# A limit on the weight bytes under way in a recurrent attention chain

## The chip, the cores and the metric

The kernel runs on one core of one Trainium2 chip. The metric is the device time of one execution in microseconds (us). The core has a matrix engine (TensorE, "PE" in the profile, its weight loads "PEld"), three engines for other arithmetic (VectorE "DVE", ScalarE "ACT", GpSimd "POOL"), and SyncE ("SP"), which here does nothing but issue transfers between the chip's memory (HBM) and the on-chip memory. SP issues the large transfers and POOL the small ones; all of them are carried by the same 16 DMA engines. A transfer that has ended raises a semaphore, and instructions wait on semaphores.

## The reference, cut to what matters

Four layers are applied in turn, A, B, A, B, each to the layer-normed rows and added to them:

```python
for s in range(n_seg):                        # layer A: 64 segments of 32 tokens
    h = concatenate([mem, x[32*s:32*s+32]])   # 8 memory rows + 32 tokens, 640 wide
    q, k, v = h @ Wq, h @ Wk, h @ Wv          # 32 heads of 192: 6144 columns each
    p = softmax(mask(q @ k.T * scale))
    o = (p @ v) @ Wo                          # back to 640 columns
    mem = o[:8]                               # the memory of the next segment
    outs.append(o[8:])
```

The eight memory rows make layer A a chain: a segment's projections can't start before the segment before it has gone through `Wo`. Layer B is a linear attention over all 2048 rows and isn't touched here. All weights are bf16; `Wq`, `Wk`, `Wv` and `Wo` together have 31.5 MB, more than the on-chip memory holds.

## The kernel before

Each A layer has two parts. `A_pre` computes the queries, keys and values of the last eight tokens of every segment ahead of time and stores them in HBM (`kqb_d`, `vb_d`). `A_chain` then runs the 64 segments one after another, in an order of instructions written out by hand on every engine.

**Rounds.** The 32 heads are taken in four rounds of eight heads, in the order 0, 1, 2, 3 in even segments and 3, 2, 1, 0 in odd ones. A round projects Q, K and V (`project`, L988; the input rows are stationary and the weights stream through), forms scores (`scores`, L1025 and L1030), weighs them (L1085, L1099, L1104 to L1106), multiplies with the values (`attend`, L1038) and goes through its quarter of `Wo` (`wo_round`, L1067: 12 steps of four matmuls, in the order of the columns of the weight tile). The sum over the four rounds is turned (L1220) and copied into the next segment's input `hT` (L1221, two copies). In what follows a segment begins at the end of the second copy.

**Streamed weights.** Most of the weights stay on chip. What doesn't fit is shared by the first and the last round of a segment: three of the five 128-row blocks of each of Q, K and V have one slot, and the tile `wo_end` holds a quarter of `Wo` for round 0 or round 3. When the first round has used a slot, SP issues the transfer that fills it for the last round. Per segment SP issues 18 transfers, always in this order, which is also the order of the names used below:

| name | tile and line of the issue | KB each |
|---|---|---|
| Q1 to Q3 | `slot["Q"]`, L681 | 384 |
| K1 to K6 (halves) | `slot["K"]`, L681 | 192 |
| V1 to V3 | `slot["V"]`, L681 | 384 |
| w1 to w6 | `wo_end` from `wo_rows`, L698 | 320 |

The transfer of a slot waits for the matmuls that read the slot before. There are also eight completion semaphores, used in turn, so a transfer waits for the one issued eight places earlier. SP takes its instructions in order. Q1 is issued 0.09 us after a segment begins, V3 at 6.8 us and w6 at 11.7 us (medians of the trace). The last round of `Wo` reads w1 to w6 in order; its matmuls 41 to 48 read w6.

**Small transfers.** POOL issues, in each segment, four loads of the precomputed values (`extra_v`, L971, `Vp<-vb`, 28 KB), four of the precomputed keys and queries (`load_kqb`, L959, 48 KB), four stores of tails (`store_tail`, L1058, 24 KB), one load of rows (L939) and one store (L955). Two tiles `Vp` are used in turn, so the load for round n + 2 is issued when `attend` of round n is done. The load for the last round, the second of the segment and called Vp1 below, is issued 12.1 us into the segment, and `attend` of the last round waits for it.

PE also fetches its own instructions by transfers of 16 KB on a queue of its own ("q8 instruction" in the page).

Of the kernel before, what the change touches and what calls it, by code (L numbers as in the profile page):

```python
# [8 lines left out]
P = 128  # L9
# [10 lines left out]

FILL = {0: 86, 2: 79}
SEG_FILL = 2

LATE = 64512
ARENA = 202752
# [90 lines left out]
class Kernel:  # L116
# [526 lines left out]
    def layer_A(self, xn_dram, at_dram, li, x_raw=None):  # L643
        nc, tc = self.nc, self.tc
        KC, NSEG = self.KC, self.NSEG
        dram = self.dram
        NR = 4
        PW = 1536
        self.kqb_d = dram.tile([NR, P, NSEG, 192], BF16, name=f"kqb{li}")
        self.vb_d = dram.tile([NSEG, NR, 2, 8, 896], BF16, name=f"vb{li}")  # L650
        self.otb_d = dram.tile([P, NSEG, 384], BF16, name=f"otb{li}")
        wview = self.wview
        wov = self.A_Wo.rearrange("h d m -> (h d) m").rearrange("(c p) m -> p c m", p=P)
        low = self.view(0, LATE)
        at = LATE
        res, slot = {}, {}
        for r in (3, 2):
            for m in "KQV":
                for b in range(KC - (SLOTS[m] if r == 3 else 0)):
                    res[m, r, b] = low[:, len(res) * PW:len(res) * PW + PW]  # L660
        assert len(res) * PW * 2 == LATE
        for m, r, b in [(m, 0, b) for m in "KQV" for b in range(KC - SLOTS[m])] + \
                [(m, None, b) for m in "KQV" for b in range(KC - SLOTS[m], KC)] + [(m, 1, b) for m in "KQV" for b in range(KC)]:
            v = self.view(at, 2 * PW)
            at += 2 * PW
            if r is None:
                slot[m, b] = v
            else:
                res[m, r, b] = v
        holds = {}  # L670
        wo_mid = self.view(at, 24 * 1280)
        wo_end = self.view(at + 24 * 1280, 12 * 1280)
        assert at + 36 * 1280 == ARENA
        unread = set(res)

        def load_slot(m, r, b, whole=False):
            if holds.get((m, b)) != r:
                holds[m, b] = r
                w = PW if whole or m in "QV" else PW // 2
                for h in range(0, PW, w):  # L680
                    nc.sync.dma_start(out=slot[m, b][:, h:h + w], in_=wview[m][:, b, PW * r + h:PW * r + h + w])  # L681

        def load_matrix(m, r):
            for b in range(KC):
                if (m, r, b) in unread:
                    unread.remove((m, r, b))
                    nc.sync.dma_start(out=res[m, r, b], in_=wview[m][:, b, PW * r:PW * r + PW])
                elif (m, r, b) not in res:
                    load_slot(m, r, b, True)

        early = {(0, 4), (0, 5), (2, 4), (2, 5), (1, 0), (1, 1), (1, 2), (1, 3)}

        def load_wo(r, into=None, part=range(6)):
            t = into if into is not None else wo_end[:, :] if r in (0, 3) else wo_mid[:, 7680 * (r - 1):7680 * r]
            for k in part:
                tk = t[:, 1280 * k:1280 * k + 1280]
                if r in (0, 3):
                    self.last_load = nc.sync.dma_start(out=tk, in_=self.wo_rows[r // 3, :, 1280 * k:1280 * k + 1280])  # L698
                else:
                    nc.sync.dma_start(out=tk.rearrange("p (c m) -> p c m", m=640),  # L700
                                      in_=wov[:, 12 * r + 2 * k:12 * r + 2 * k + 2, :])

        def piece(m, r, b):
            assert (m, r, b) in res or holds[m, b] == r
            return res[m, r, b] if (m, r, b) in res else slot[m, b]

        if li == 0:
            self.wo_rows = dram.tile([2, P, 7680], BF16, name="wo_rows")

        def lay_out_wo(i):  # L710
            nc.sync.dma_start(out=self.wo_rows[i].rearrange("p (c m) -> p c m", m=640), in_=wov[:, 36 * i:36 * i + 12, :])

        def early_wo():
            for r in (2, 0, 1):
                load_wo(r, part=[k for k in range(6) if (r, k) in early])

        def late_wo(r, part=range(6)):
            load_wo(r, part=[k for k in part if (r, k) not in early])

        self.A_pre(xn_dram, li, load_matrix, piece, wo_mid, wo_end, lay_out_wo, early_wo, x_raw)  # L720
        self.A_chain(xn_dram, at_dram, li, load_slot, piece, load_wo, late_wo, wo_mid, wo_end, low)
        self.post_args = at_dram, wo_mid, wo_end, low

# [192 lines left out]
    def A_chain(self, xn_dram, at_dram, li, load_slot, piece, load_wo, late_wo, wo_mid, wo_end, low):  # L916
# [3 lines left out]
        with tc.tile_pool(name=f"A{li}_ch", reuse_waits="tile", bufs=1) as sp, \  # L920
# [150 lines left out]
            def keep_busy(ps, n, w=384):  # L1071

                for _ in range(n):
                    nc.tensor.matmul(ps[:, 0:w], lhsT=self.ident[:, :], rhs=wo_mid[:, 0:w], start=True, stop=True,  # L1074
                                     skip_group_check=True)

            def fill(n):

                for _ in range(n):
                    nc.tensor.ldweights(self.ident[:, 0:1])  # L1080
# [40 lines left out]
            for s in range(NSEG):  # L1121
# [93 lines left out]
                keep_busy(idle, 5, 230)  # L1215
                fill(SEG_FILL)
                if s + 1 < NSEG:
# [87 lines left out]
```

## Time and profile before

| | us |
|---|---|
| median of three runs (3610.51 to 3611.67) | 3610.64 |
| span of the profiled execution, first to last instruction | 3590.5 |
| what lies around the span (no time of its own is listed for the profiled execution, so this is against the median) | 20.1 |
| 62 segment periods of the first A layer and 62 of the second, in sum | 2621.6 |
| mean, median and fastest twentieth of a segment period | 21.14, 21.01, 20.71 |

The two chains take 73% of the span. PE is marked busy for 97% of the span, but that share says little: matmuls are pipelined and a dependent step shows as a gap of tenths of a microsecond. What matters is which event ends last before each step of a segment, so the chain of work that ended last, the waits and the landing times of transfers are read segment by segment.

### The profile page before, as it was taken

The numbers are of one execution on the slowest core, as the hardware profiler recorded it, in microseconds if no ns is written. First come the engines' busy times: TensorE is split into PE (matmuls) and PEld (weight loads), VectorE is DVE, ScalarE is ACT, GpSimd is POOL, SyncE is SP. The second block draws the span as 40 slices with busy tenths as digits, with TensorE's granted clock in tenths as the row PEclk, the third lists the DMA queues.
The fourth block names the chain that finished last, engine by engine and source line by source line (L and its number), as shares of the span: only waits on it lengthen the run. The fifth ranks groups of instructions, "written<-read, shape, count | busy, mean of one in ns | idle before, by whom it ended". The sixth has DMA issues, their size and how long they took to land.

```text
span 3590.5 us, 168460 instructions
## 1 busy us (share of the span) xinstructions
PE 3465.5 (97%) x70978; PEld 2268.6 (63%) x71399; DVE 2327.0 (65%) x6320; ACT 2032.0 (57%) x5233; POOL 1589.1 (44%) x4173
## 2 busy tenths in 40 slices
PE   9989999999999999999999899999999999999999
PEld 7756666666666666655377566666666666666553
DVE  5466666667666666746633566666666666676465
ACT  3356666666566656646432556666666666666463
POOL 3445555555555555530123455555545555555400
PEclk9999999999999999999999999999999999999999
DMA  8988888888788878860476878887888888888600
GB/s 311 334 290 288 281 295 282 278 292 299 278 284 295 289 277 278 295 224 3 146 272 217 290 275 287 290 291 278 285 294 279 290 282 292 292 281 287 222 1 30
DMA packets 452689, 929.38 MB, mean 259 GB/s; under 512 B 75338, under 2 KB 218330, under 8 KB 448858
## 3 DMA queue, kind: packets, MB, share of 16 engines
q1 hardware_dynamic: 382266, 817.56, 64.0%
q0 software_dynamic: 67744, 87.80, 7.9%
q8 instruction: 557, 9.13, 1.0%
q10 hardware_dynamic: 1920, 13.24, 0.9%
q14 instruction: 202, 1.65, 0.1%
HBM read 848.50 MB, written 73.73 MB: 257 GB/s over the span
## 4 chain that ended last, share of the span: by engine, by line
PE 55%; DMA 20%; issue 9%; DVE 7%; POOL 5%; ACT 4%; SPq 1%; PEld 0%; POOLq 0%; ACTq 0%; DVEq 0%
PE ps_qk L988 17%; DMA arena<-wo_rows 7%; DMA Vp<-vb 6%; PE ps_v L988 6%; PE ps_w L1067 6%; PE ps_pre L878 3%; PE ps_o L1038 3%; PE ps_s L1030 3%; DVE hT L943 2%; PE ps_s L1099 2%; DMA arena<-in_A_Wv_dram 2%; PE ps_s L1025 2%; PE ps_pre L902 2%; PE ps_idle L1074 2%; PE kv L1260 1%
## 5 line engine op out<-in xcount | busy, mean ns | idle before, releaser
L988 PEld LDWEIGHTS <-hT 128*32 128x32 bf16 x30720 | 746.5, 96 | 431.9 <-DVE hT L1221 27.2
L988 PE MATMUL ps_qk<-arena,hT 128*32 128x384 bf16 x20480 | 998.8, 328 | 14.6 <-DMA arena<-in_A_Wq_dram 4.2
L998 ACT ACTIVATE raw<-ps_qk 128x384 bf16<-128x384 f32 x1024 | 502.0, 490 | 383.7 <-PE ps_s L1099 250.9
L988 PE MATMUL ps_v<-arena,hT 128*32 128x384 bf16 x10240 | 534.6, 328 | 8.7 <-DMA arena<-in_A_Wv_dram 8.4
L971 POOL DMA_DIRECT2D Vp<-vb x512 | 258.4, 505 | 611.4 <-PE ps_o L1038 465.6
L1067 PE MATMUL ps_w<-arena,OT 128*32 128x160 bf16 x18432 | 446.1, 234 | 11.4 <-DMA arena<-wo_rows 10.4
L1003 DVE STREAM_TRANSPOSE KT<-raw 128x384 bf16<-128x384 bf16 x512 | 296.0, 578 | 194.5 <-ACT raw L998 190.5
L1067 PEld LDWEIGHTS <-OT 128*32 128x32 bf16 x18432 | 322.7, 96 | 103.8 <-ACT OT L1044 22.3
L1006 DVE STREAM_TRANSPOSE QT<-raw 128x256 bf16<-128x256 bf16 x512 | 227.9, 445 | 237.5 <-ACT raw L998 195.5
L959 POOL DMA_DIRECT2D kqb<-kqb x512 | 290.9, 568 | 168.9 <-POOL KT L967 147.3
L1019 DVE CAST Vp<-ps_v 64x384 bf16<-64x384 f32 x512 | 286.2, 559 | 113.6 <-ACT Vp L1017 90.0
L1106 DVE TENSOR_TENSOR E<-E,ps_s 80x320 bf16<-80x320 bf16 x512 | 247.4, 483 | 142.7 <-ACT ps_s L1105 142.3
L1058 POOL DMA_DIRECT2D otb<-otb x512 | 282.7, 552 | 128.1 <-DVE otb L1054 100.0
L1017 ACT ACTIVATE Vp<-ps_v 64x384 bf16<-64x384 f32 x512 | 246.1, 481 | 138.4 <-PE ps_v L988 122.9
L1038 PEld LDWEIGHTS <-Vp 80*128 80x128 bf16 x4096 | 189.9, 99 | 123.1 <-issue 80.5
L1038 PE MATMUL ps_o<-E,Vp 80*128 80x80 bf16 x4096 | 233.0, 201 | 31.8 <-DMA Vp<-vb 15.0
L1085 ACT ACTIVATE E<-ps_s 80x320 bf16<-80x320 f32 x512 | 221.4, 432 | 68.0 <-PE ps_s L1030 33.6
L951 ACT ACTIVATE Vp<-ps_w 32x160 bf16<-32x160 f32 x512 | 150.3, 294 | 155.1 <-DVE wt L1220 138.4
L964 POOL COPY QT<-kqb 128x64 bf16<-128x64 bf16 x512 | 124.5, 243 | 254.8 <-PE ps_s L1030 248.5
L1030 PE MATMUL ps_s<-QT,KT 128*80 128x80 bf16 (+1 forms) x3072 | 233.2, 213 | 1.6 <-POOL KT L967 1.5
L1104 ACT ACTIVATE ps_s<-ps_s 80x320 f32<-80x320 f32 x512 | 214.7, 419 | 31.2 <-PE ps_s L1099 31.2
L1030 PEld LDWEIGHTS <-KT 128*80 128x80 bf16 x3072 | 205.4, 119 | 28.7 <-issue 18.3
(156 smaller groups left out, 5446.4 us busy)
## 6 DMA issues: line engine op xcount, KB each, us to landing
arena<-wo_rows SPq DMA_DIRECT2D x780, 320.0 KB, 6.8
arena<-in_A_Wq_dram SPq DMA_DIRECT2D x427, 384.0 KB, 4.4
arena<-in_A_Wv_dram SPq DMA_DIRECT2D x427, 384.0 KB, 6.6
arena<-in_A_Wk_dram SPq DMA_DIRECT2D x768, 192.0 KB, 4.6
kqb<-kqb POOLq DMA_DIRECT2D x512, 48.0 KB, 5.1
arena<-in_A_Wk_dram SPq DMA_DIRECT2D x43, 384.0 KB, 7.8
vb<-arena POOLq DMA_DIRECT2D x128, 112.0 KB, 6.3
Vp<-vb POOLq DMA_DIRECT2D x512, 28.0 KB, 4.8
```

The lines of the kernel that those rows point to most:

```text
L959: nc.gpsimd.dma_start(out=kqb[:], in_=self.kqb_d[r, :, s, :])
L971: nc.gpsimd.dma_start(out=Vs[n % 2][64:80, :], in_=self.vb_d[s, r].rearrange("g t f -> (g t) f"))
L988: nc.tensor.matmul(o[32 * g:32 * g + 32, 0:384], lhsT=hT[:, b, :], rhs=rhs, start=(i == 0), stop=(i == KC - 1), tile_position=(0, 32 * g), ...
L998: nc.scalar.activation(out=raw[:], in_=ps[:, 0:384], func=ACT.Copy)
L1003: nc.vector.transpose(out=KT[:, :, 0:64], in_=raw[:, :].rearrange("p (c j) -> p c j", j=64))
L1017: nc.scalar.activation(out=o, in_=i, func=ACT.Copy)
L1019: nc.vector.tensor_copy(out=o, in_=i)
L1030: nc.tensor.matmul(S[0:80, c0:c0 + 80 * (q1 - q0)], lhsT=KT[:, 3 * x + i, :], rhs=QT[:, x, q0:q1, :], start=False, stop=(x == 1 and i == 2 ...
L1038: nc.tensor.matmul(O[x][:, 80 * i:80 * i + 80], lhsT=Vs[n % 2][0:80, 448 * x + k:448 * x + k + 128], rhs=E[0:80, 160 * x + 80 * e:160 * x ...
L1058: nc.gpsimd.dma_start(out=self.otb_d[:, s, 96 * r:96 * r + 96], in_=otb[:, :, :].rearrange("p c t -> p (c t)"))
L1067: nc.tensor.matmul(W[32 * g:32 * g + 32, 0:160], lhsT=OT[:, c, q:q + 32], rhs=w[:, 640 * i + 160 * g:640 * i + 160 * g + 160], start=(firs ...
L1106: nc.vector.tensor_tensor(out=E[0:80, 0:320], in0=E[0:80, 0:320], in1=rc, op=ALU.mult)
```

## The change

Inside `A_chain`, each transfer of a streamed weight is entered in a list with its bytes. Going back from the newest one, the bytes are added up, its own included; the first transfer with which the sum passes 1,310,720 bytes (1.25 MB) must have completed before the new one is issued. The wait stands on SP, ahead of the issue. Transfers of `A_pre`, of resident weights and of layer B aren't entered, nor are POOL's. The order of instructions is the same on every engine.

```diff
+FLIGHT = 1310720
...
         holds = {}
+        under_way = []
+        self.pacing = False
+
+        def stream(out, in_, nbytes):
+
+            load = nc.sync.dma_start(out=out, in_=in_)
+            if self.pacing:
+                under_way.append((load.ins, nbytes))
+                total = 0
+                for ins, n in reversed(under_way):
+                    total += n
+                    if total > FLIGHT:
+                        tc.add_manual_dep(load.ins, ins.name,
+                                          mybir.DependencyInfo(mybir.DependencyClass.Sync, mybir.DependencyReason.DATA),
+                                          reason="few streamed weights under way")
+                        break
+            return load
+
...
                 for h in range(0, PW, w):
-                    nc.sync.dma_start(out=slot[m, b][:, h:h + w], in_=wview[m][:, b, PW * r + h:PW * r + h + w])
+                    stream(slot[m, b][:, h:h + w], wview[m][:, b, PW * r + h:PW * r + h + w], 2 * P * w)
...
                 if r in (0, 3):
-                    self.last_load = nc.sync.dma_start(out=tk, in_=self.wo_rows[r // 3, :, 1280 * k:1280 * k + 1280])
+                    self.last_load = stream(tk, self.wo_rows[r // 3, :, 1280 * k:1280 * k + 1280], 2560 * P)
...
         self.A_pre(xn_dram, li, load_matrix, piece, wo_mid, wo_end, lay_out_wo, early_wo, x_raw)
+        under_way.clear()
+        self.pacing = True
         self.A_chain(xn_dram, at_dram, li, load_slot, piece, load_wo, late_wo, wo_mid, wo_end, low)
```

With the sizes of the table the rule gives these pairs, a transfer and the one that it waits for: K1 and K2 for Q1, K3 and K4 for Q2, K5 and K6 for Q3, V1 for K2, V2 for K4, V3 for K6, w1 for V1, w2 for V2, w3 and w4 for V3, w5 for w1, w6 for w2. Q1 to Q3 wait for w4 to w6 of the segment before.

## The prediction

> **What bounds the kernel now.** I read the chain that ended last first: it tells which events a segment waits for. From the page:
>
> ```profile
> span 3590.5 us, 168460 instructions
> PE 55%; DMA 20%; issue 9%; DVE 7%; POOL 5%; ACT 4%; SPq 1%; PEld 0%; POOLq 0%; ACTq 0%; DVEq 0%
> PE ps_qk L988 17%; DMA arena<-wo_rows 7%; DMA Vp<-vb 6%; PE ps_v L988 6%; PE ps_w L1067 6%; PE ps_pre L878 3%; PE ps_o L1038 3%; PE ps_s L1030 3%; DVE hT L943 2%; PE ps_s L1099 2%; DMA arena<-in_A_Wv_dram 2%; PE ps_s L1025 2%; PE ps_pre L902 2%; PE ps_idle L1074 2%; PE kv L1260 1%
> ```
>
> Two transfers stand high: the `Wo` tiles (w1 to w6) and POOL's small `Vp<-vb`. The chain in order of time (start, us, what) shows a segment of each sort:
>
> ```profile
> 1042.09 6.03 DMA Vp<-vb
> 1048.16 0.47 PE ps_o L1038 x8
> ...
> 578.01 8.80 DMA arena<-wo_rows
> 586.82 0.04 issue
> 586.86 0.32 PE ps_w L1067 x8
> ```
>
> In the first, `attend` of the last round starts 0.04 us after Vp1 lands; in the second, the last eight `Wo` matmuls start 0.04 us after w6 lands. The waits of PE put the visible idle time beside it (engine, line, releaser, us, times, longest):
>
> ```profile
> PE ps_w L1067 <- issue: 16.4, 36, 1.2
> PE ps_o L1038 <- DMA Vp<-vb: 15.0, 39, 1.0
> PE ps_w L1067 <- DMA arena<-wo_rows: 10.4, 23, 1.0
> ```
>
> SP's waits show that the weights are held by slots more than by transfers:
>
> ```profile
> SPq L681 <- PE ps_qk L988: 1191.2, 365, 11.4
> SPq L698 <- PE ps_w L1067: 294.7, 245, 2.7
> SPq L681 <- DMA arena<-in_A_Wq_dram: 79.3, 139, 3.4
> SPq L1230 <- DMA otb<-otb: 10.5, 2, 5.5
> ```
>
> The windows of one segment (us, five engines, clock, DMA share, GB/s) show the DMA engines full for 13 us and nearly idle for 4:
>
> ```profile
> 1013.00:1026.00 13.00, 12.65 (x310) 8.04 (x298) 9.27 (x25) 9.11 (x25) 7.15 (x23) 1.00 1.03 377
> 1026.00:1030.00 4.00, 3.89 (x125) 3.14 (x127) 3.11 (x11) 0.81 (x4) 2.54 (x6) 1.00 0.32 100
> ```
>
> From the trace's start and landing times over 124 segment periods I take, in us after the segment's begin: Vp1 lands at 17.88 (median) and `attend` starts 0.05 later in 76 of 118 segments. Without that wait it could start at 17.69, after the last normalising multiply (L1106, end 17.64). From there 0.88 to the first `Wo` matmul, 0.70 to the 41st, which needs w6, 1.22 to 1.30 to the next segment. w6 lands at 19.57 (median; 18.91 to 20.28 for nine in ten) and the 41st matmul starts 0.04 later in 45 of the 94 segments whose w6 landing is recorded. So a period is
>
> 41st matmul = the later of (ready for `attend` + 1.58) and (w6 + 0.04), then about 1.25 more.
>
> The 41st matmul starts at 19.88 on average. Both gates are live in most segments; moving one only uncovers the other.
>
> **The change, part by part.**
>
> *It binds.* Bytes outstanding at Vp1's issue (12.14) are V2, V3 and w1 to w6, 2.75 MB by their landings; after the change 1.31 MB at most.
>
> *Small transfers get faster.* The four `Vp<-vb` loads of a segment are issued with 1.97, 2.75, 1.31 and 0.33 MB of weights outstanding and take 5.69, 5.71, 3.78 and 1.92 us (medians). Under the cap Vp1 lies nearest to the third: 3.8 us, landing near 15.9. The ends are 1.92 (no backlog) and 5.71 (no help). Anything under 5.50 us frees `attend`, so its lateness, 21.8 us in sum over the 124 periods, goes. What is late next is w6.
>
> The Trainium skill's page "DMA: Bandwidth & Descriptors", section "Queues, rings and completion order", says that a DMA engine goes round its queues packet by packet, so that a small transfer on a queue of its own would not stand behind another queue's backlog, and the cap would gain it nothing. The four rows above disagree: the same 28 KB takes three times as long with 2 to 2.75 MB outstanding.
>
> *PE's instruction fetches.* Of PE's gaps with releaser "issue" at L1067, 29 (14.8 us in the chains, where the gap is over 0.25 us) begin after an instruction packet that the trace shows at 14.5 to 15.7, at the peak of the backlog. I treat these as a fetch that queues like Vp1, and let them go too (ends: 0 and 14.8 us).
>
> With both gone, readiness + 1.58 averages 19.40. If w6 stayed where it is, the later of the two, segment by segment, would lie 0.16 us before today's 19.88: 124 x 0.16 = 20 us gained.
>
> *w6 lands later by x.* Packets of Q and V take 121 ns, of K 65, of wo 102, eight per engine and transfer. The first starts 0.64 us after the issue ends, a landing follows the last packet by 0.55 us, and SP's issue ends 0.22 us after its wait: 1.41 us from a transfer's last packet to the first of the one that waits for it. Taking today's landings, each gated transfer's data could start, against when its packets are served today (landing minus 0.55 minus eight packets):
>
> K1: Q1 lands 3.85 + 0.86 = 4.71, served 5.63, spare 0.92. K5: Q3 6.19 + 0.86 = 7.05, served 7.80, spare 0.75. V1: K2 7.24 + 0.86 = 8.10, served 10.02, spare 1.92. w2: V2 12.67 + 0.86 = 13.53, served 14.24, spare 0.71. w3: V3 13.69 + 0.86 = 14.55, served 15.31, spare 0.76. w6: w2 15.61 + 0.86 = 16.47, served 18.20, spare 1.73.
>
> So on the engine that finishes last, no wait is late: x = 0 is one end. But a landing is that of the slowest of 16 engines, and the others run dry before it. The 16 packets of one Vp1, one per engine, start over 1.43 us (1066.81 to 1068.24): an engine that is ahead by so much idles up to 1.43 - 0.71 = 0.72 us at a gate. If it is next delayed itself (an instruction packet occupies one engine for 1.0 us, some four a segment), the lost time reaches w6. That is the other end: 0.7. Below nothing, evening out the engines might bring at most some 0.3. I take the middle of 0 and 0.7, x = 0.35, since rows support both the spare and the spread and neither is nearer. DMA share 1.03 leaves no idle time in which to recover.
>
> Then the later of the two averages 0.14 us after 19.88: 124 x 0.14 = 17.6 us lost. Each further 0.1 us of x costs about 11 us; the break-even is x = 0.2. Because w6 rules by then, it hardly matters how much Vp1 gains: without any gain there it would be 24.9.
>
> The same page's section "Anatomy of one DMA — SWDGE (gpsimd) path" puts the fixed cost of a transfer near 2 us. Put in place of the 1.41 us it would use up 0.6 of the spare of 0.7, and the middle estimate would be x near 0.65, or 53 us lost; the packets say 1.41.
>
> *Other deadlines and SP's queue.* V3 lands at 13.69 and is read at 14.5. I expect it 0.1 to 0.2 later, which costs only in segments past 14.5 today (one in twenty lands after 14.69): 1 us in sum. K6 (10.05, read near 13) and Q3 (6.19, read near 11) have 3 us and more of cover; without it each would cost like w6. Behind a waiting SP instruction stand only further weight transfers and, in the last segment, the two fetches of L1230, which wait for the tails' stores anyway. No compute engine waits for SP except through those landings. Chain starts and ends: four paced `Wo` transfers per layer, bounded by 0 and 2 us a layer; I take 0, as they stand behind older transfers.
>
> *Sum.* Against the profiled span: 3590.5 + 17.6 + 1 = 3609.1; with the 20.1 us around it, 3629.2, say 3629 against the median of 3610.6 (the execution's own time isn't listed beside its span).
>
> **The rivals.**
>
> *The other side: w6 doesn't move.* One mechanism: the same engine is last at gate after gate, so the spare of 0.71 or more covers every wait. x = 0 gives the 20 us of above: 3591. It decides below x = 0.2. For it: every spare is positive. Against it: the spread of 1.43 us is twice the smallest spare. Chance 0.30.
>
> *The two cancel.* x between 0.12 and 0.27 lies within 7 us of 3611. Chance 0.15.
>
> *No help for small transfers.* Their delay would come not from weights outstanding in the queue but from what each engine has already taken in, which 1.31 MB still fills. Vp1 stays late, x = 0.35: 24.9 us, 3636. Against it the third `Vp<-vb`, 3.78 us at 1.31 MB. Chance 0.07. This is also what packet-by-packet turns would give.
>
> *Starved stream.* Idle at more than one gate of a segment adds up, between one loss of 0.72 and two (1.44); at x = 1.0 the formula gives 95 us: 3706. Against it the spares of V1 and w6 (1.9 and 1.7), where losses are taken back. Chance 0.10.
>
> **How the numbers follow.** The forecast (x 0.27 to 0.6, 3619 to 3658) has 0.38. About 0.2%, 7 us, can be told from no change. Faster 0.30; within 0.15; slower 0.38 + 0.07 + 0.10 = 0.55. The range runs from x = 0 and a little below (3588) to x = 0.8, about 3680; the starved stream beyond it and x under -0.05 are left out. Slower cases alone: 3619 to 3706.
>
> **What would show it.** Right: `Vp<-vb` at 3.5 to 4.5 us, landing by 17 in nearly all segments; its waits at L1038 and the "issue" gaps at L1067 nearly gone; PE's wait for `arena<-wo_rows` several times today's 10.4 us; w6 at 19.9; DMA share below 1 between 13 and 18 us; wo_rows' landing time down from 6.8 to near 4 us though w6 is later. Wrong: w6 at or before 19.6 with the waits for `Vp<-vb` gone (faster), or V3 after 14.5 (slower still, with waits at L988 on `arena<-in_A_Wv_dram`).

## The result and the profile after

The changed kernel takes 4165.66 us (median of four runs, 4154.47 to 4172.84) against 3611.15 us: a ratio of 1.152 (95% interval 1.150 to 1.155). 555 us are lost; 18 were forecast, and the range ended at 3680.

From the page of the changed kernel: its span, PE's busy time, the chain that ended last by engine and by line, and the median times from issue to landing of two transfers.

```profile
span 4166.7 us, 168458 instructions
...
PE 3696.3 (89%) x70978; PEld 2370.7 (57%) x71399; DVE 2326.2 (56%) x6320; ACT 2020.2 (48%) x5233; POOL 1589.1 (38%) x4173
...
DMA 46%; PE 42%; issue 3%; ACT 3%; DVE 3%; PEld 2%; SPq 0%; POOL 0%; ACTq 0%; DVEq 0%; POOLq 0%
DMA arena<-wo_rows 24%; PE ps_qk L1010 14%; DMA arena<-in_A_Wv_dram 13%; DMA arena<-in_A_Wk_dram 5%; PE ps_v L1010 4%; PE ps_w L1089 3%; PE ps_pre L900 3%; PE ps_idle L1096 2%; DMA arena<-in_A_Wq_dram 2%; PE ps_s L1052 2%; PE kv L1282 2%; PE ps_s L1121 1%; PE ps_o L1060 1%; PE ps_pre L924 1%; PE ps_s L1047 1%
...
arena<-wo_rows SPq DMA_DIRECT2D x780, 320.0 KB, 4.6
...
Vp<-vb POOLq DMA_DIRECT2D x512, 28.0 KB, 4.1
```

DMA rises from 20% of the chain (718 us) to 46% (1917 us), and it is the streamed weights; `Vp<-vb`, 6% before, is no longer in the list. Most single transfers are faster than before (6.8 to 4.6 us for `Wo`, 6.6 to 4.7 for V, 4.6 to 4.1 for the halves of K; Q alone went from 4.4 to 4.6), yet the stream as a whole is later. The lines of code have moved by about 20: L988 is now L1010, L1067 is L1089, and every streamed transfer is issued at L678.

PE's waits (engine, line, releaser, us, times, longest):

```profile
PE ps_w L1089 <- DMA arena<-wo_rows: 255.0, 297, 3.1
PE ps_v L1010 <- DMA arena<-in_A_Wv_dram: 151.6, 196, 3.3
```

Before they were 10.4 us (shown above) and 8.4 us:

```profile
PE ps_v L988 <- DMA arena<-in_A_Wv_dram: 8.4, 9, 3.2
```

SP's own waits show where the time is spent instead:

```profile
SPq L678 <- PE ps_qk L1010: 712.8, 424, 18.4
SPq L678 <- DMA arena<-wo_rows: 461.0, 276, 5.2
SPq L678 <- DMA arena<-in_A_Wv_dram: 456.7, 384, 4.7
SPq L678 <- DMA arena<-in_A_Wk_dram: 409.0, 351, 4.3
SPq L678 <- DMA arena<-in_A_Wq_dram: 302.3, 273, 3.2
```

Some 1630 us of waits for landings, where the kernel before had about 200, the largest next to the 79.3 us shown above being

```profile
SPq L681 <- DMA arena<-in_A_Wv_dram: 71.2, 115, 1.3
```

The chain in order of time (start, us, what) shows one segment's end:

```profile
1222.97 0.58 PE ps_w L1089 x25
1223.55 5.95 DMA arena<-in_A_Wv_dram
1229.49 0.02 issue
1229.51 0.03 SPq L678
1229.53 0.03 issue
1229.56 3.13 DMA arena<-wo_rows
1232.69 0.02 issue
1232.71 0.02 SPq L678
1232.73 0.03 issue
1232.76 5.16 DMA arena<-wo_rows
1237.91 0.04 issue
1237.96 0.32 PE ps_w L1089 x8
```

V2 lands, which lets w2 go; w2 lands, which lets w6 go; w6 lands and the last eight `Wo` matmuls start. Landing, issue, landing, with nothing of PE in between. The windows of the same segment (us, five engines, clock, DMA share, GB/s):

```profile
1224.00:1231.00 7.00, 5.37 (x122) 3.15 (x114) 3.68 (x10) 3.23 (x10) 3.00 (x8) 1.00 0.69 211
1228.00:1230.50 2.50, 0.91 (x32) 0.42 (x21) 1.06 (x2) 0.77 (x3) 1.11 (x2) 1.00 0.35 110
1231.00:1237.00 6.00, 5.78 (x137) 4.75 (x136) 3.40 (x10) 2.31 (x7) 2.97 (x8) 0.72 0.81 280
```

Where the DMA engines ran at 377 GB/s before, they now fall to 211 and, for 2.5 us, to a third of their time: from 1228.5 to 1230.5 the trace has one or two weight packets under way at a time, seldom three, so one or two engines finish their parts while the others have none left. A fetch of PE's instructions held one engine from 1226.89 to 1227.85, just before; whether it was the one that is late, the trace doesn't tell. The third line also shows the granted clock at 0.72.

Landings in us after a segment's begin (medians of the trace over 124 periods):

| | Q1 | K2 | K6 | V1 | V3 | w1 | w4 | w6 | Vp1 | mean period |
|---|---|---|---|---|---|---|---|---|---|---|
| before | 3.85 | 7.24 | 10.05 | 11.54 | 13.69 | 14.85 | 17.66 | 19.57 | 17.88 | 21.14 |
| after | 4.00 | 8.05 | 11.72 | 12.78 | 16.52 | 17.56 | 21.88 | 24.22 | 17.04 | 25.66 |

The delay grows all along the stream, and 124 x 4.52 = 561 us is the whole loss. The chain of gates K2, V1, w1, w5 lands at 8.05, 12.78, 17.56 and 22.87: 4.7 to 5.3 us from one landing to the landing of the transfer that waited for it, in which 1.2 MB pass. At 377 GB/s they would take 3.2 us. Against the kernel before, the landings of Q1, K2, V1, w1 and w5 are late by 0.15, 0.81, 1.24, 2.71 and 4.38 us: each round adds its own loss.

From the first weight packet of a segment to the last it is 17.94 us before and 22.54 us after. Of that an average engine is idle for 1.08 and 3.56 us, and busy for 16.86 and 18.97 us. Of the busy time the weights, 5.5 MB in both, take 15.3 and 16.8 us; most of the rest is POOL's small transfers, of which more fall into the longer stretch. So of the 4.6 us that the stretch grew, 2.5 are idle time and 1.5 slower weight packets.

The packets of 3072 bytes take 0.139 us on average before and 0.152 after, with a median of 0.121 in both. The slow ones gather after a lull. In the changed kernel, where at no time 0.1 to 0.4 us earlier more than four engines were busy, 63% of the weight packets take more than 1.5 times the usual, with 15 or more busy 6%; 176 weight packets a segment start with fewer than 15 engines busy in that time, against 46 before the change. It is the packets of 3072 bytes above all (0.36 us in the median after such a lull, nearly all of them in the first 2 us of a segment); those of `Wo` keep their median (0.105 against 0.102 us), and 29% of them are slow. Why is not shown.

### The profile page after: what moved, and what is told of

Its sections match the earlier page's. It is cut to its first block, busy times and chain, and to the rows that moved or that the text cites. A ratio compares the mean times of both kernels' runs of the same rounds, so it can differ in the third digit from the quotient of the medians.

```text
span 4166.7 us, 168458 instructions
## 1 busy us (share of the span) xinstructions
PE 3696.3 (89%) x70978; PEld 2370.7 (57%) x71399; DVE 2326.2 (56%) x6320; ACT 2020.2 (48%) x5233; POOL 1589.1 (38%) x4173
## 4 chain that ended last, share of the span: by engine, by line
DMA 46%; PE 42%; issue 3%; ACT 3%; DVE 3%; PEld 2%; SPq 0%; POOL 0%; ACTq 0%; DVEq 0%; POOLq 0%
DMA arena<-wo_rows 24%; PE ps_qk L1010 14%; DMA arena<-in_A_Wv_dram 13%; DMA arena<-in_A_Wk_dram 5%; PE ps_v L1010 4%; PE ps_w L1089 3%; PE ps_pre L900 3%; PE ps_idle L1096 2%; DMA arena<-in_A_Wq_dram 2%; PE ps_s L1052 2%; PE kv L1282 2%; PE ps_s L1121 1%; PE ps_o L1060 1%; PE ps_pre L924 1%; PE ps_s L1047 1%
## 5 line engine op out<-in xcount | busy, mean ns | idle before, releaser
L1010 PEld LDWEIGHTS <-hT 128*32 128x32 bf16 x30720 | 780.5, 100 | 675.9 <-issue 281.8
L1010 PE MATMUL ps_qk<-arena,hT 128*32 128x384 bf16 x20480 | 1076.3, 347 | 12.4 <-DMA arena<-in_A_Wk_dram 6.6
L1089 PE MATMUL ps_w<-arena,OT 128*32 128x160 bf16 x18432 | 512.0, 240 | 256.1 <-DMA arena<-wo_rows 255.0
L1010 PE MATMUL ps_v<-arena,hT 128*32 128x384 bf16 x10240 | 579.9, 333 | 152.3 <-DMA arena<-in_A_Wv_dram 151.6
L1089 PEld LDWEIGHTS <-OT 128*32 128x32 bf16 x18432 | 336.4, 97 | 396.0 <-issue 331.7
L1060 PEld LDWEIGHTS <-Vp 80*128 80x128 bf16 x4096 | 201.2, 102 | 95.1 <-issue 81.1
L1060 PE MATMUL ps_o<-E,Vp 80*128 80x80 bf16 x4096 | 243.7, 206 | 11.3 <-DVE E L1128 0.2
L1096 PE MATMUL ps_idle<-arena,ident 128*128 128x230 bf16 (+1 forms) x1792 | 246.9, 274 | 0.0
L1242 DVE STREAM_TRANSPOSE wt<-ps_w 128x96 f32<-128x96 f32 x252 | 65.1, 259 | 309.9 <-PE ps_w L1089 309.8
```

The lines of the kernel that those rows point to most:

```text
L1010: nc.tensor.matmul(o[32 * g:32 * g + 32, 0:384], lhsT=hT[:, b, :], rhs=rhs, start=(i == 0), stop=(i == KC - 1), tile_position=(0, 32 * g), ...
L1060: nc.tensor.matmul(O[x][:, 80 * i:80 * i + 80], lhsT=Vs[n % 2][0:80, 448 * x + k:448 * x + k + 128], rhs=E[0:80, 160 * x + 80 * e:160 * x ...
L1089: nc.tensor.matmul(W[32 * g:32 * g + 32, 0:160], lhsT=OT[:, c, q:q + 32], rhs=w[:, 640 * i + 160 * g:640 * i + 160 * g + 160], start=(firs ...
```

## The experiments

All times stand against the kernel before, run on the same chip. Where no interval is given, the run is a single one; the four runs of the changed kernel lie within 0.4% of each other. Theory A is that the stream starves: bytes under way, divided by the time from issue to landing, is less than the segment needs. Theory B is that each wait on SP has a price of its own. Later the question is what makes the round so long.

### How many bytes, and which transfers

```diff
-FLIGHT = 1310720
+FLIGHT = 1572864
```

> The limit is 1.5 MB (four transfers of 384 KB) in place of 1.25 MB (three), all else as in the changed kernel. Theory A, the stream is starved: from one landing to that of the transfer that waited for it, the trace after has 4.7 to 5.3 us for 1.2 MB, of which 3.3 us are data at the 377 GB/s of before, so some 1.4 us a round go to the issue, the first packet and the engines that ran ahead of the slowest. One transfer more (0.97 us of packets) covers most of it: some 0.4 us a round are left in four rounds, w6 about 1.5 us late, near 3770 us. Theory B, each wait on SyncE has a price of its own (15 of them, 0.3 us each): as many waits stand there, 4100 us or more.

3750.15 us against 3597.89: 1.042. w6 lands at 21.07, 1.5 us late, as theory A had it.

```diff
-FLIGHT = 1310720
+FLIGHT = 1966080
```

> The limit is 1.875 MB (five transfers of 384 KB). Theory A: 1.9 us more of packets than with three, more than the 1.4 us that were uncovered: w6 within 0.5 us of before, 3600 to 3670 us, and the small load Vp1 still earlier than before. Theory B (a price per wait): 4100 us or more.

3561.67 us against 3597.89, faster than the kernel before and than expected. The same waits stand on SP as in the changed kernel, so theory B falls. PE's waits in this kernel:

```profile
PE ps_w L1089 <- DMA arena<-wo_rows: 20.6, 50, 1.5
...
PE ps_v L1010 <- DMA arena<-in_A_Wv_dram: 8.7, 9, 3.5
```

The waits for `Vp<-vb` are down from 15.0 to 0.3 us; Vp1 lands at 16.79 and w6 at 19.44.

Since this beats both kernels, it was timed again, with a larger limit beside it.

> The kernel with the limit of 1.875 MB once more, timed in rounds. In its first look every segment's w6 landed at 19.44 us (19.57 before) and Vp1 at 16.8 (17.88 before), and the mean period was 20.87 us against 21.14: 124 x 0.27 = 33 us of 3600, 0.9%. If that is the limit's doing, the ratio to the kernel before is 0.988 to 0.994; if the look was luck, 0.997 to 1.003.

3585.05 us against 3619.24: 0.990 (0.988 to 0.992). The gain is real.

```diff
-FLIGHT = 1310720
+FLIGHT = 2293760
```

> The limit is 2.19 MB (seven Wo transfers). Theory A (starved below about 1.6 MB, and small transfers that queue behind the weight bytes under way): the stream is never starved, Vp1 lies between 16.8 (1.875 MB) and 17.88 us (2.75 MB): about 17.3, still before attend is ready in most segments, so 0.990 to 0.996 of the time before. If small transfers were freed by the waits and not by the bytes, as much as at 1.875 MB.

3589.12 us against 3619.24: 0.992 (0.991 to 0.994), Vp1 at 17.58 us. The small load's time goes with the bytes under way: 3.5 us at a limit of 1.0 MB (below), 4.2 at 1.25 and 1.5 MB, 4.65 at 1.875, 5.42 at 2.19, 5.71 with 2.75 MB and no limit.

```diff
-FLIGHT = 1310720
+FLIGHT = 1048576
```

> The limit is 1.0 MB (two transfers of 384 KB, three of 320 KB, five of 192 KB). Theory A as a rate: bytes under way over the time from issue to landing. Between landings 1.0 MB on average under a limit of 1.25 MB and 4.6 us gave 214 GB/s from Q1's to w6's landing, 1.2 MB under 1.5 MB gave 252 GB/s. With 0.8 MB and 4.4 us it is about 180 GB/s, so 4.33 MB take 24 us and w6 lands near 28: period 29.3 us, 124 x 8.1 = 1010 us over the kernel before: 4500 to 4900 us. If the loss has levelled off (one bad gate a segment): 4200 us.

4361.79 us against 3596.23: 1.213, above the changed kernel but below the 4500 that was expected. w6 lands at 25.87, not 28. The rate was taken with a time of 4.4 us from issue to landing; with less under way it is shorter (2.9 us for K6 and V3, 3.5 for w1, from the end of the issue), so the rate falls more slowly than the bytes. The expectation also counted 4.33 MB from Q1's landing to w6's. By the sizes of the table it is 5.11 MB, and the rates are 232, 253 and 295 GB/s at limits of 1.0, 1.25 and 1.5 MB; the formula's fit to the two rates it was built on was an accident.

The next two keep the limit for one kind of transfer.

```diff
-            if self.pacing:
+            if self.pacing and nbytes == 2560 * P:     # wo_only; qkv_only: !=
```

> The 1.25 MB limit is kept for the Wo transfers alone; Q, K and V are issued as before. Of a segment's waits two are left that can bind: w5 for w1 and w6 for w2. Theory A: w1 landed at 14.85 us before, w5's data could start at 15.7 and was served at 17.1, so nothing binds: 3595 to 3640 us. Theory B: two waits of 0.3 us: 3680 us.

3614.59 us against 3597.89: 1.005, inside the range of theory A. Vp1 comes 0.38 us earlier (17.50), w6 0.1 us later in the median (19.66) but 0.65 us later at its slowest twentieth (20.93), and I read this as what takes the gain away. PE's waits:

```profile
PE ps_w L1089 <- DMA arena<-wo_rows: 40.3, 43, 2.0
```

> The 1.25 MB limit is kept for Q, K and V alone; the Wo transfers are issued after V3 without a wait for landings beyond the eight semaphores. Theory A: V3 lands 2.8 us late as in the changed kernel (16.5 us into a segment); w1 to w6 then follow at the full rate, 5.2 us for 1.97 MB, so w6 lands near 21.9, 2.3 us late: near 3890 us. Theory B: 9 waits of 0.3 us, 2.7 us: 3940 us. If the loss sits in the Wo waits alone: near 3630 us.

3911.31 us against 3597.89: 1.087. V3 lands at 15.97 and w6 at 21.97, where 21.9 was expected. PE waits in both places:

```profile
PE ps_v L1010 <- DMA arena<-in_A_Wv_dram: 165.4, 196, 2.8
PE ps_w L1089 <- DMA arena<-wo_rows: 97.5, 153, 2.3
```

So the greater part of the loss is made among Q, K and V, by transfers that wait for each other in a row of gates; `Wo` alone has only two gates that can bind.

### The grain

```diff
             load = nc.sync.dma_start(out=out, in_=in_)
...
+            if self.pacing and nbytes > 196608:
+                w = out.shape[-1] // 2
+                stream(out[:, 0:w], in_[:, 0:w], nbytes // 2)
+                return stream(out[:, w:2 * w], in_[:, w:2 * w], nbytes // 2)
```

(The new lines stand ahead of the issue.)

> The limit stays 1.25 MB, but each transfer of 384 or 320 KB is issued as two of half the columns, each with its own wait. Theory A: a new piece may start when half a transfer has landed, so on average about 0.1 MB more is under way; between 1.25 MB (4166 us) and 1.5 MB (3750 us) 0.1 MB is worth some 160 us: near 4000 us. Theory B (a price per wait or per transfer on SyncE, now 27 instead of 15 waits): 4300 us or more. If the coarse grain of three transfers were the whole trouble: below 3750 us.

4089.5 us against 3619.24: 1.130, where the changed kernel has 1.152. A finer grain gives back 2%, about half of the 160 us that theory A allowed. (The edit makes 24 waits where there were 15, not 27.) Theory B, which asked for 4300 us or more, falls a second time.

### What makes the round long

PE's clock first. The trace has its granted share at 0.5 in 118 stretches, 99 of them of 3.4 us, 486 us in sum; 109 lie inside the chains, where the kernel before has one. The Trainium skill's page "TensorE: Matmul & The Clock Gate", section "Part 1: The HAM clock gate", says that PE falls to half its clock after an idle window of about 3.4 us and takes as long to come back; the length of the stretches agrees. The idle window does not: in the 124 periods PE has no gap longer than 3.1 us, and in the 3.4 us before a stretch begins there PE, its weight loads included, was busy for 18 to 67% (median 47%). Here a window of which PE idled half was enough.

```diff
+            def wide(W, n):
+                for _ in range(n):
+                    nc.tensor.matmul(W[:, 160:512], lhsT=self.ident[:, :], rhs=wo_mid[:, 0:352], start=True, stop=True,
+                                     skip_group_check=True)
...
                 wo_round(W, order[L - 2], OT1, False, False, range(6))
+                wide(W, 12)
...
+                wide(W, 10)
                 wo_round(W, order[L], OT, False, True)
```

> The changed kernel with 12 wide matmuls (128x352, nothing reads them) ahead of the last round's streamed V blocks and 10 ahead of the last round of Wo, where PE idles for some 2.5 and 1.8 us a segment. The trace after shows the granted clock at 0.5 for 3.4 us at a time, 115 times or so; before, it stood at 1.0 throughout the chains. If the fallen clock is what costs the time, keeping PE busy brings back most of it: below 3900 us. If the transfers end last and the clock only follows from the idle time, nothing or little is gained: 4120 to 4200 us, with the clock up.

The wide matmuls begin new sums in the bank that holds Wo's, so this kernel doesn't compute the reference. 4054.2 us against 3619.24: 1.120. The clock is up:

```profile
core 0: 4052.5 us, clock 0.993
```

w6 lands at 23.29 instead of 24.22. So the clock had a part in the loss, about a fifth (some 3 of 15%, net of what the added matmuls cost), more than the "little" of one answer and far less than the "most" of the other.

Next the instruction fetches. A landing is that of the last of 16 engines, and the trace has the time at which each engine ends its part. In the changed kernel the last engine ends 0.75 us after the eighth where no fetch of PE's instructions overlaps the transfer, and 1.37 us after it where one does (means); each fetch of 16 KB lasts 1.08 us, and there are 4.0 in a segment. The trace doesn't name the engines, so it doesn't show that the late one is the one that fetched.

```diff
-                wo_round(W, order[L - 2], OT1, False, False, range(6))
+                wide(W, 3)
...
-                wo_round(W, order[L - 2], OT1, False, False, range(6, 8))
+                wide(W, 1)
...
-                wo_round(W, order[L - 2], OT1, False, False, range(8, 12))
+                wide(W, 2)
...
-                wo_round(W, order[L - 1], OT, False, False)
+                wide(W, 7)
```

Its base on the same chip:

> The changed kernel once more, as the base on this chip for the next two: 4140 to 4180 us.

4131.15 us against 3596.23: 1.149, a little under the range given.

> The changed kernel with the Wo products of the second and third round left out; in their place 13 wide matmuls (128x352, unread) of about the same time. PE issues 166 instructions fewer a segment, so it fetches 16 KB some 0.6 times less often out of 4. If an instruction fetch, which holds one of the 16 engines for about 1 us, is what makes an engine the slowest one at a gate (in the trace after, the last engine ends 1.37 us behind the eighth where a fetch overlaps, 0.75 us where none does), each fetch less saves up to 0.62 us: up to 0.4 us a segment, 20 to 50 us in all. If the spread comes from elsewhere: no difference to the changed kernel beyond 10 us.

3989.17 us: 142 us under its base, three times what a fetch's effect on one landing had promised. Fetches are 3.35 a segment. But the clock's stretches at 0.5 also fell, from 97 to 68, so two causes are mixed here. And the segments of this run tell against the number of fetches: the 80 with three fetches take 24.22 us on average, the 44 with four 24.31 (standard errors 0.08 and 0.11). Those with four, as many as every segment of the base has, are still 1.05 us shorter than the base's 25.37.

The same edit at the limit of 1.875 MB:

> The same products left out, at the limit of 1.875 MB, where the stream isn't starved: the fetches' delay is hidden by the transfers queued behind, so 0.985 to 0.993 of the kernel before, as with the products. If leaving them out shortens PE's own work by itself: below 0.98.

3586.79 us against 3596.23: 0.997, a little slower than with the products (0.990 there). With enough under way fewer fetches bring nothing. The five runs with the products, on another chip, lie 0.6% apart, so the difference to them isn't clear of noise.

The last three were to take the two causes apart.

> The changed kernel as the base on this chip: 4130 to 4175 us.

4152.48 us against 3609.22: 1.151.

```diff
+            def same(W, part):
+                for i in part:
+                    for g in range(4):
+                        nc.tensor.matmul(W[32 * g:32 * g + 32, 160:320], lhsT=self.ident[:, 0:32],
+                                         rhs=wo_mid[:, 640 * i + 160 * g:640 * i + 160 * g + 160], start=True, stop=True,
+                                         tile_position=(0, 32 * g), skip_group_check=True)
...
-                wo_round(W, order[L - 2], OT1, False, False, range(6))
+                same(W, range(6))
...
-                wo_round(W, order[L - 1], OT, False, False)
+                same(W, range(12))
```

> The control to the run with fewer instruction fetches (3989 us against 4131 on its chip): the Wo products of the second and third round are replaced by as many matmuls of the same shape that read nothing of the round and write unread columns. PE issues as many instructions, so it fetches as often. If the fetches made the 142 us: within 40 us of the base. If it was the missing dependence on the round's result, or the products' reads: as fast as with fewer fetches, 3960 to 4020 us.

4156.41 us, 4 us from the base: neither the products nor their dependence matter.

```diff
-                wo_round(W, order[L - 2], OT1, False, False, range(6))
...
-                wo_round(W, order[L - 2], OT1, False, False, range(6, 8))
...
-                wo_round(W, order[L - 2], OT1, False, False, range(8, 12))
...
-                wo_round(W, order[L - 1], OT, False, False)
```

> The Wo products of the second and third round are left out with nothing in their place: 192 instructions fewer a segment (0.7 fetches of 4) and some 2 us less of PE work, so more idle time and no wide matmuls that hold the clock up. If the fetches made the 142 us: 3950 to 4050 us. If the wide matmuls did, by the clock: at the base or above it.

4072.47 us, 80 us under the base, although the clock is much lower. The instruction queue (packets, MB, share of 16 engines' span) on the page of the base:

```profile
q8 instruction: 557, 9.13, 0.9%
```

and on the page of this kernel, whose mean granted clock is 0.885 where the base has 0.948:

```profile
q8 instruction: 461, 7.55, 0.8%
```

The mean period falls from 25.56 to 24.90 us for 0.76 fetches less a segment. Read as a price that is 0.86 us for a fetch, but the price isn't shown. Within this run the 94 segments with three fetches take 24.76 us and the 30 with four 25.36, yet those with four also ran longer at half clock (7.9 against 6.5 us a segment), and in the run with wide matmuls the two sorts hardly differ. PE's own work is also 2 us shorter here; with the transfers ending last, and the control at the base, I don't read the gain as that, but it isn't excluded. So fewer instructions on PE do shorten the starved kernel, by 80 and 142 us; whether by the number of fetches, by where in a segment they fall, or otherwise is open. What the waits, the issue, the spread of the engines and the lull cost apart was not separated either.

## Why the prediction was wrong, point by point

**It binds, and small transfers get faster.** Right in the mechanism, though the changed kernel alone wouldn't show it. Vp1 takes 4.2 us (3.8 forecast); it is issued 1.0 us later than before, at 13.14, and lands at 17.04, where 15.9 was forecast. Its waits at L1038 are gone and so are the "issue" gaps of the `Wo` matmuls, 16.4 us before, but both would be hidden in any case: `attend` of the last round, held up by V3, starts 3.0 us after Vp1. The proof is the limit of 1.875 MB, where V3 is on time, Vp1 lands at 16.8 and the two waits are down to 0.3 and 1.1 us. The step against packet-by-packet turns stands: the limits from 1.0 to 2.19 MB give times from 3.5 to 5.4 us.

**The formula of a period.** Right. In the changed kernel the 41st matmul starts 0.04 us after w6 in the median, and the segment ends 1.22 to 1.36 us later.

**x, the delay of w6.** This is the term that failed: 4.65 us, where 0.35 was taken between 0 and 0.7. Two steps in it were wrong. The first: "on the engine that finishes last, no wait is late", from spares of 0.71 us and more. The spares compared medians of landings at six of the gates, each for itself, with the transfers ahead in the queue taken to be on time. The second: "an engine that is ahead by so much idles up to 1.43 - 0.71 = 0.72 us at a gate", counted once a segment. The runs show losses that add up along the gates instead of ending in one: 0.15 us at Q1, 0.81 at K2, 1.24 at V1, 2.71 at w1, 4.38 at w5. In the stream of a segment an average engine idles for 2.5 us more than before, where at most 0.7 was allowed, and the weight packets take 1.5 us more, which the prediction had at nothing. That too few bytes under way are the cause is shown by the row of limits, from 1.213 at 1.0 MB to 0.990 at 1.875 MB. What makes each round so long, the spread of the engines, the fetches or the slow packets, is my reading of the traces and not separated.

The spread could have been read before. The sixteen completions of each transfer in the trace of before lie 1.2 us apart for Q and K (1.9 for K6) and 2.2 to 2.4 us for V and `Wo`, and the last comes 0.8 to 1.9 us behind the eighth; I had looked at one small transfer. The Trainium skill's page "DMA: Bandwidth & Descriptors", section "Why a DMA increments its semaphore by 16 and not by 1", says that the engines of a DMA finish independently and only the full count means that all has landed; these rows agree, and a gate on a landing is therefore a barrier over the engines.

**Starved stream.** The right kind of answer stood among the rivals with a chance of 0.10, at x = 1.0 and 95 us. I had set it aside for the spares of V1 and w6, "where losses are taken back". They weren't. K2, the gate of V1, came only 0.8 us late, less than the spare of 1.9, but V1 also stands behind K3 to K6 in SP's order, and these landed 1.7 to 2.2 us late; V3 came 2.8 us late.

**The fixed cost.** Of the 1.41 us two parts held: after the change 0.63 us from the end of the issue to the first packet and 0.47 to 0.50 from the last packet to the landing. The third didn't: SP's issue ends 0.39 us after the landing it waits for, not 0.22, and 0.87 us after it where two transfers wait for the same landing, since SP issues them in turn; the prediction left these second ones (K2, K4, K6, w4) out. 0.2 us a gate would still have left every listed spare above 0.5 us. The 2 us of the Trainium skill's section named in the prediction (it is on POOL's path, while SP issues these transfers), put in place of the 1.41, would have given 53 us: the right direction, but a tenth of the loss.

**Other deadlines.** V3 was to come 0.1 to 0.2 us late at 1 us in sum; it comes 2.83 us late, past the 14.5 at which it is read, and PE waits 151.6 us for `Wv`.

**PE's clock.** Not in the prediction at all. It fell as PE waited longer, which was worth about a fifth of the loss.

**The other side.** x = 0 with 20 us gained wasn't this limit's result but is close to that of 1.875 MB: w6 at 19.44 to 19.57, Vp1 freed, 1.0% or some 34 us faster (0.8 to 1.2%). The mechanism that spoke for the change is real; 1.25 MB is below what the stream needs.

**The base of the sum.** I put 20.1 us around the span. The changed kernel's profiled run took 4168.45 us with a span of 4166.7: 1.8 us around it. The kernel before, too, has 1.7 us around it where both are listed (3597.89 and 3596.2). The 20 us were the distance of the profiled execution from the median of the others.

## What to carry to other kernels

A limit on transfers under way is a rate limit: bytes under way over the time from issue to landing, with the time measured to the landing, which is the last engine's, and with the limit in force. Before setting one, read from the trace how far the engines' ends of one transfer lie apart; a chain of gates pays for that at every gate. How much more must be under way was found here by trying, not worked out: 1.25 MB lost 15%, 1.875 MB gained 1%. Spares worked out gate by gate from medians don't hold in a chain of gates, because each late landing moves the next.

## What was not expected of the hardware

PE's instruction fetches run beside other transfers: 16 KB hold one of the 16 DMA engines for 1.0 to 1.1 us, and a transfer that one overlaps ends 1.37 us behind its eighth engine instead of 0.75; what a fetch costs a segment stayed open. Weight packets of 3072 bytes that start after a lull take three times as long (0.36 us in the median against 0.121). The clock fell without any idle time of 3.4 us. And an optimum lies close to a cliff: 1.875 MB gives 0.990, 1.5 MB 1.042, 1.25 MB 1.152, 1.0 MB 1.213.
